# Attention and a routed MoE in one kernel: first scale, table zeros, sums, table steps, values and exponentials moved in program order

## The chip, the cores and the metric

The kernel runs on one core of a Trainium2 chip, in one launch. The metric is the device time of one execution in microseconds (us); lower is better. The core's engines work side by side, each through its own queue in program order, and wait for one another through semaphores: PE (TensorE: matrix products and transposes; its weight loads are listed apart, as PEld), ACT (ScalarE), DVE (VectorE), POOL (GpSimd) and SP (SyncE, which here only issues DMA transfers). DMA transfers are issued from SP, ACT or POOL and move data between device memory and the on-chip buffer.

## The reference

```python
def _attn_ref(q, k, v, cap):                    # q, k, v: (4, 12, 448, 64), float32
    scores = np.matmul(q, k.transpose(0, 1, 3, 2)) / np.sqrt(64)
    scores = cap * np.tanh(scores / cap)
    attn = np.exp(scores - scores.max(-1, keepdims=True))
    attn = attn / (attn.sum(-1, keepdims=True) + 1e-09)
    return np.matmul(attn, v)

def _moe_ref(x, w_gate, w_output_gate, w1, w2):  # x: (1792, 768), 8 experts, F = 1024
    logits = x @ w_gate
    e_idx = np.argmax(logits, axis=1)
    gate_w = softmax(logits)[rows, e_idx]        # abridged
    eom = 1.0 / (1.0 + np.exp(-(x @ w_output_gate)))
    for e in range(8):                           # each row goes through its own expert alone
        mask = e_idx == e
        ye = np.maximum(x[mask] @ w1[e], 0.0) @ w2[e]
        out[mask] = gate_w[mask, None] * eom[mask, e, None] * ye
```

`x` is the attention's output, laid out as one row of 12 heads x 64 for each of the 4 x 448 positions.

## The kernel before

**Attention.** The work is cut into 24 units (`NU`), six for each of the four batches; a unit is two heads. A unit `u` goes through these steps. Its keys and queries are turned so that the head dimension lies on the partitions, and split into a high and a low plane (`K..H`, `K..L`, `QH`, `QL`): a copy (the high plane) and a subtraction (the low plane, `minus`). Units 0 to 2 are turned by PE (`nat_k`, `nat_q`, which read `raw2`), all later ones by DVE (`t_k`, `t_q`, line 288); `TURN` says how many of these turns stand in a unit ahead of its exponential and how many behind. `qk(u, s)` makes four tiles of scores in a ring of three banks, and ACT takes tanh of each into `pt` (line 393, with the scale `icap`). `expo(u)` takes the exponential of the whole unit on ACT (line 396). `pv(u)` multiplies by the values `vv` on PE (line 404) and `u_evac` copies the product out. `presum(u, 0)` and `presum(u, 1)` add a unit's exponentials up in four instructions (lines 413, 414 and twice 418) for the denominators; they run on POOL, for units 20 and later on DVE. `sums` finishes them on PE. `pt` has two buffers, so the tanh of unit `u + 2` overwrites the exponentials of unit `u` and waits until `pv(u)` and `presum(u)` have read them.

**The order of the work** is written out by hand (`manual_schedule`): each engine runs its instructions in the order in which the loop over `u` emits them. In a unit: `load_v`, `qk`, turns, `presum(u - 1, 1)`, slots f and g, `expo(u)`, slot h, `pv(u - 1)`, `sums`, slot q, `u_evac(u - 1)`, turns, `presum(u, 0)`, slot e. The slots hold the steps of the batch that ended before (`end_of_batch`): denominators, gate products, logits, choice of the expert (`choose`), rank among the rows of one expert (`rank_mm`, `place`, `place2`), the weight of a row (`enter`), `scatter` (which enters each row into tables `tabs` in device memory), and six times `row_tr`, `row_out` (the attention's rows, scaled and stored to `xs` by SP). The slots of batch 2 fall into units 19 to 23.

**From attention to MoE.** `early()` is six steps of small DVE instructions that turn the counts of batches 0 to 2 into the experts and table offsets of the first five blocks of 128 rows (`meta`). After it SP reads `meta` and issues `fetch_dma` (the table's entries, `tc`), `load_raw` (the expert's weights into `raw1`, `raw2`); POOL adds the entries up and gathers the block's rows (`gather`, `xg`, line 864). In the last units `first_hi` and `first_lo` split the first weight tile on DVE. PE then turns the first block (`tx(0)`, line 876), ACT and DVE split it (`xh`, `xl`, lines 877 and 878) and every weight tile (lines 1062 and 1063), and PE multiplies (line 1084). The last batch's own steps (`STEPS`) are strewn between the chunks of the first MoE products.

**At the start** SP and ACT load unit 0, DVE fills constants (lines 198 to 203, 256 to 259), and `first_planes` makes the planes of unit 0; `scales` makes `icap`. After unit 0's last scores POOL issues `load_wg` (the gates' weights) and `clear_tabs` (five transfers of zeros from `tabi` to `xs` and the tables).

Of the kernel before, what the change touches and what calls it, by code (L numbers as in the profile page):

```python
# [22 lines left out]
def tile_kernel(ctx: ExitStack, tc, q, k, v, cap, w_gate, w_ogate, w1, w2, out):  # L23
    nc = tc.nc
    B, H, S, D = q.shape
    NT, DM = out.shape
# [3 lines left out]
    NP = H // 2  # L30
    NU = B * NP
# [3 lines left out]
    NE = 5  # L35
# [14 lines left out]
    for i, kind in enumerate((2, 4)):  # L50
# [6 lines left out]
    SP0 = 3  # L57
    UACT = 8
    TURN = {0: (0, 0), 1: (0, 0), 3: (2, 1), 5: (2, 1), 6: (2, 1), 7: (2, 1), 9: (2, 1), 10: (1, 0), 11: (1, 0), 13: (2, 1),
            14: (2, 1), 15: (2, 1), 16: (1, 0), 17: (1, 0), 19: (1, 0), 20: (1, 0), 21: (0, 0)}  # L60
    KD = DM // 128
    KF = DFF // 128
    PB = 5
# [35 lines left out]
    NK = 3  # L99
# [72 lines left out]
    def scales():  # L172
        nc.vector.reciprocal(out=icap, in_=capc)
        nc.vector.tensor_scalar(out=icap, in0=icap, scalar1=float(D) ** -0.5, scalar2=None, op0=ALU.mult)

        nc.vector.tensor_scalar(out=epsc, in0=capc, scalar1=-1.0, scalar2=None, op0=ALU.mult)
        nc.vector.tensor_tensor(out=epsc, in0=epsc, in1=capc, op=ALU.min)

# [14 lines left out]


    ohc = rtp.tile([128, NP, 32], F32, name="ohc")
    nc.vector.memset(ohc, 0.0)
    for p in range(NP):
        nc.vector.memset(ohc[:, p, p:p + 1], 1.0)  # L200

    wg = rtp.tile([128, NP, 2, 16], F32, name="wg")
    nc.vector.memset(wg, 0.0)

    def load_wg():
        for j in range(2):
# [8 lines left out]
    onesb = rtp.tile([CP, 128], BF16, name="onesb")  # L215
    nc.gpsimd.memset(onesb, 1.0)
    tabi = rtp.tile([128, NTAB // 128, 2], F32, name="tabi")

    def clear_tabs():
        nc.gpsimd.dma_start(out=xs[NT:NT + 8].rearrange("r (a m) -> (r a) m", a=16),  # L220
# [33 lines left out]
        nc.gpsimd.memset(wrow[:, 1, COL[r]], 128.0 / KIND[r] - 64.0)  # L254

    part = const.tile([128, 4], F32, name="part")
    for g in range(4):
        for z, x in enumerate((2 * NT + g // 2, 4 * NT + g, 6 * NT + g, 6 * NT + 4 + g)):
            nc.vector.memset(part[32 * g:32 * g + 32, z:z + 1], float(x))
    ereg = const.tile([1, E], F32, name="ereg")  # L260
    nc.gpsimd.iota(ereg, pattern=[[REG, E]], base=128, channel_multiplier=0,
                   allow_small_or_imprecise_dtypes=True)
# [9 lines left out]
    pl, pt, ut, s1, ups, smt, rec, xr, lg = {}, {}, {}, {}, {}, {}, {}, {}, {}  # L272

    def copy(act, dst, src):
        if act:
            nc.scalar.activation(out=dst, in_=src, func=ACTF.Copy)
        else:
            nc.vector.tensor_copy(out=dst, in_=src)
# [4 lines left out]
    def minus(out, x, y):  # L283
        nc.vector.tensor_tensor(out=out, in0=x, in1=y.bitcast(F32), op=ALU.subtract)
# [6 lines left out]
    def q_parts(u, ps):  # L291
        hi, lo = part_tile("QH", [128, S]), part_tile("QL", [128, S])
        return [hi, lo], [(hi, lo, ps)]

    def k_parts(u, ps):
        hi, lo = kpl[u % PB]
        parts = [(hi[:, 0:SK], lo[:, 0:SK], ps[:, 0:SK])]
        for j in range(2):
            h, c = slice(64 * j, 64 * j + 64), slice(SK + 64 * j, SK + 64 * j + 64)
            parts.append((hi[h, c], lo[h, c], ps[h, SK:S]))  # L300
        return [hi, lo], parts

    def planes_of(made):
        ts, parts = made
        for x, _, y in parts:
            copy(False, x, y)
        for x, z, y in parts:
            minus(z, y, x)
        return ts

    def first_planes(pk, pq):
        k_, (main, *tails) = k_parts(0, pk)
        q_, (q0,) = q_parts(0, pq)
        copy(True, main[0], main[2])
        copy(True, q0[0], q0[2])
        for x, z, y in (main, q0):
            minus(z, y, x)
        for x, z, y in tails:
            copy(False, x, y)
            minus(z, y, x)  # L320
        return k_ + q_

    def t_k(u):
        pl[u] = planes_of(k_parts(u, turned(ldk.pop(u), S)))
# [32 lines left out]
    def nat_k(u):  # L357
        pk = tbank([128, S], "tk0")
        for c in range(NK + 1):
            n = min(128, S - c * 128)  # L360
            nc.tensor.transpose(pk[:, c * 128:c * 128 + n], nat[u][0][0:n, c].rearrange("p j d -> p (j d)"), ident[0:n, 0:n])
        return pk

    def nat_q(u):
        pq = scores("tq0")[:, 0, 0:S]
        for c in range(NCH):
            nc.tensor.transpose(pq[:, c * CP:(c + 1) * CP], nat[u][1][:, c].rearrange("p j d -> p (j d)"), ident[0:CP, 0:CP])
        return pq

    def prep_first():  # L370
        pk = nat_k(0)
        pl[0] = first_planes(pk, nat_q(0))
        scales()

    def qk(u, s):
        KH, KL, QH, QL = pl[u]
# [79 lines left out]
    def end_of_batch(b):  # L456
# [82 lines left out]
        def rank_mm():  # L539

            ps = rt["ps"] = bank([128, 2, NCH, E], "trk")
            ohf = rt["ohb"].rearrange("p c e -> p (c e)")
            nc.tensor.matmul(ps[0:CP, 0].rearrange("p c e -> p (c e)"), lhsT=tri, rhs=ohf, start=True, stop=True)
            nc.tensor.matmul(ps[:, 1].rearrange("p c e -> p (c e)"), lhsT=onesb, rhs=ohf, start=True, stop=True)
            den = rt["den"]
            nc.scalar.activation(out=T("ex"), in_=rt["d"], func=ACTF.Exp)
            nc.scalar.activation(out=den[:, 1], in_=den[:, 1], func=ACTF.Exp, scale=-1.0)
# [59 lines left out]
        L = lambda *fs: (lambda: [f() for f in fs])  # L607
        P = lambda f, *a: (lambda: f(*a))
        rws = [L(P(row_tr, p), P(row_out, p)) for p in range(NP)]
        t = [sums_out, L(sums_tr, recips), L(P(gate_mm, 0), P(gate_out, 0)), L(P(gate_mm, 1), P(gate_out, 1))]  # L610
        gts = [L(P(gate_tr, g), P(gate_mul, g)) for g in range(2)]
        g0, g1 = t[2], t[3]
        if b < B - 2:
            at = {(-2, "q"): [g0], (0, "q"): [g1], (0, "e"): [sums_out], (1, "g"): [t[1]],
                  (2, "g"): [rws[0], rws[1]], (3, "g"): gts, (3, "h"): [logits], (4, "g"): [rws[2], rws[3]], (4, "h"): [choose],
                  (5, "g"): [rank_mm, place, rws[4]], (5, "h"): [place2, enter], (6, "g"): [rws[5]]}
            for i, x in enumerate(((6, "g"), (8, "g"), (9, "g"), (10, "g")) if b == 0 else ((6, "g"),) * NCH):
                at.setdefault(x, []).append(P(scatter, (i,)))
        elif b == B - 2:
            g = early()  # L620
            nx = P(next, g, None)
            lds = [P(load_raw, 0, w, c) for w in range(2) for c in range((KD, KF)[w])]
            fd = [P(fetch_dma, i) for i in range(NE)]
            at = {(-2, "q"): [g0], (0, "f"): [P(sums, EARLY), g1, sums_out], (0, "h"): [t[1], *gts, logits, choose],
                  (1, "g"): [rws[0], rank_mm, place], (1, "h"): [place2, enter, scatter], (1, "q"): [rws[1], rws[2], rws[3], store_rows],
                  (1, "e"): [nx] * 5,
                  (2, "g"): [rws[4], rws[5]], (2, "h"): [nx, P(set_known, NE), store_rows],
                  (2, "q"): [fd[0], fd[1], *lds[:2]],
                  (3, "h"): [P(gather, 0), P(gather, 1), *lds[2:4]], (3, "e"): [fd[2], fd[3], *lds[4:KD]], (4, "f"): lds[KD:]}
        if b < B - 1:  # L630
            for (x, y), fs in at.items():
                for f in fs:
                    slots.setdefault((NP * (b + 1) + 1 + x, y), []).append(f)
            return
        nx = P(next, late_steps, None)
        do = dict(g=t[2], s=L(P(sums, NU - 1), t[0]), S=t[1], G=t[3], x=gts[0], X=gts[1], l=logits, c=choose, r=rank_mm, p=place, q=place2,
                  e=enter, n=nx, z=L(P(set_known, NSLOT), P(fetch_dma, NE)), h=lambda: next(rests(), None))
        do.update({str(p): rws[p] for p in range(NP)})
        return [L(*[do[x] for x in w]) for w in STEPS.split()]
# [320 lines left out]
    def slot(u, y):  # L960
        for f in slots.pop((u, y), ()):
            f()

    prep_first()
    warm(WARM[1])
    load_ahead(NN + 1)
    slots.setdefault((2, "f"), []).append(eps)

    for u in range(NU):
        if u % 2:  # L970
            load_v(u + 1)
        for s in range(NK):
            qk(u, s)
        if u == 0:
            pl[1] = planes_of(k_parts(1, nat_k(1)))
        if u > 0:
            load_ahead()
        qk(u, NK)
        if u == 0:
            pl[1] += planes_of(q_parts(1, nat_q(1)))  # L980
            nc.vector.memset(tabi, 0.0)
            load_wg()
            clear_tabs()
        if u == 1:
            pl[2] = planes_of(k_parts(2, nat_k(2)))
            pl[2] += planes_of(q_parts(2, nat_q(2)))
        before, after = TURN.get(u, (2, 0))
        turn_next(before)
        if 0 < u <= NU - 4:
            presum(u - 1, 1)  # L990
        slot(u, "f")
        slot(u, "g")
        expo(u)
        if u > NU - 4:
            presum(u - 1, 0)
            presum(u - 1, 1)
        slot(u, "h")
        if u > 0:
            for c in range(NK + 1):
                pv(u - 1, c)  # L1000
        if u > 1 and u - 2 != EARLY:
            sums(u - 2)
        slot(u, "q")
        if u > 0:
            u_evac(u - 1)
        turn_next(after)
        if u < NU - 4:
            presum(u, 0)
        slot(u, "e")
        store_rows()  # L1010
    u = NU - 1
# [348 lines left out]
```

## Time and profile before

| what | us |
|---|---|
| median of 3 runs (514.47 to 514.91) | 514.79 |
| the profiled execution | 514.19 |
| its span, first to last instruction | 512.6 |
| PE busy | 488.6 (95%) |
| DVE busy | 381.3 (74%) |
| ACT busy | 371.7 (73%) |
| POOL busy | 288.8 (56%) |

The profiled execution took 1.6 us more than its span. Shares are means over two very different stages: attention runs to about 202 us, the MoE from there to the end. The mean granted clock of TensorE is 0.994 of full speed.

### The profile page before, as it was taken

How to read it: one execution, taken by the hardware profiler on the slowest of the kernel's cores; microseconds unless marked ns; L12 is line 12 of the kernel's file. 1: busy time of each engine (PE TensorE's matmuls, PEld its weight loads, DVE VectorE, ACT ScalarE, POOL GpSimd, SP SyncE). 2: the span in 40 equal slices, each digit the busy share in tenths (PEclk: the TensorE clock that was granted, in tenths of full speed). 3: DMA queues.
4: the chain of work that ended last, by engine and by line, in shares of the span. 5: the costliest groups of instructions: out<-in, count | busy, mean ns of one | idle time of the engine just before them, and what ended most of it. 6: DMA issues, size and time to landing. Idle time of an engine off the chain costs nothing. (4 is left out here: it accounts for less than half of the span.)

```text
span 512.6 us, 10021 instructions
## 1 busy us (share of the span) xinstructions
PE 488.6 (95%) x3069; PEld 341.1 (67%) x3069; DVE 381.3 (74%) x746; ACT 371.7 (73%) x433; POOL 288.8 (56%) x310
## 2 busy tenths in 40 slices
PE   7899999999999988999999999999999999999994
PEld 6444455444545543678989979988788867686691
DVE  7669999798686897988999878867676857555550
ACT  5888988889887868556589878858676867665551
POOL 4999998888988614962268861317265035352001
PEclk9999999999999989999999999999999999999998
DMA  6879868484532548884099336259759689991001
GB/s 144 168 134 162 142 108 144 91 146 83 87 70 49 86 61 287 316 271 130 2 350 407 115 104 245 62 207 368 272 191 394 263 308 362 336 359 67 1 33 49
DMA packets 152380, 91.92 MB, mean 179 GB/s; under 512 B 135027, under 2 KB 135163, under 8 KB 152321
## 3 DMA queue, kind: packets, MB, share of 16 engines
q1 hardware_dynamic: 142336, 58.24, 43.6%
q0 software_dynamic: 8832, 32.74, 17.3%
q8 instruction: 26, 0.43, 0.4%
q10 hardware_dynamic: 1152, 0.25, 0.2%
q14 instruction: 34, 0.27, 0.2%
HBM read 123.68 MB, written 12.04 MB: 265 GB/s over the span
## 5 line engine op out<-in xcount | busy, mean ns | idle before, releaser
L1063 DVE TENSOR_TENSOR wr<-raw,wr 128x768 fp32r<-128x768 f32 (+1 forms) x167 | 172.8, 1073 | 64.4 <-ACT wr L1062 63.5
L1062 ACT ACTIVATE wr<-raw 128x768 fp32r<-128x768 f32 (+1 forms) x167 | 150.6, 936 | 28.1 <-PE py L1084 12.4
L393 ACT ACTIVATE pt<-s,icap 128x896 f32<-128x896 f32 x96 | 80.1, 914 | 17.1 <-PE s L386 9.9
L404 PE MATMUL u<-pt,vv 128*64 128x448 f32 x384 | 79.1, 555 | 1.5 <-ACT pt L393 1.1
L1084 PE MATMUL py<-wr,hh 128*128 128x384 f32 x352 | 77.3, 340 | 0.0
L1084 PE MATMUL php<-wr,xh 128*128 128x512 f32 x264 | 74.8, 404 | 0.0
L1153 POOL DMA_INDIRECT out_dram<-yo,ti x13 | 21.7, 1668 | 90.8 <-ACT yo L1151 67.4
L396 ACT ACTIVATE pt<-pt,capc 128x3136 f32<-128x3136 f32 x24 | 69.9, 2912 | 0.6
L1084 PEld LDWEIGHTS py<-wr,hh 128*128 128x128 f32 x352 | 61.2, 188 | 4.0 <-issue 3.7
L1084 PEld LDWEIGHTS php<-wr,xh 128*128 128x128 f32 x264 | 47.4, 188 | 12.8 <-issue 2.5
L418 POOL TENSOR_TENSOR pb<-pb,pt 64x448 f32<-64x448 f32 x42 | 49.6, 1181 | 10.1 <-DVE pb L414 7.0
L404 PEld LDWEIGHTS u<-pt,vv 128*64 128x64 f32 x384 | 25.9, 139 | 42.6 <-issue 34.7
L413 POOL TENSOR_TENSOR pa<-pt 128x896 f32<-128x896 f32 x20 | 42.3, 2114 | 10.8 <-ACT pt L396 10.0
L1084 PE MATMUL py<-wr,hl 128*128 128x384 f32 x176 | 44.8, 335 | 0.0
L414 POOL TENSOR_TENSOR pb<-pa,pt 128x896 f32<-128x896 f32 x20 | 42.1, 2103 | 1.6
L1084 PE MATMUL php<-wr,xl 128*128 128x512 f32 x132 | 41.6, 396 | 0.9 <-DVE xl L878 0.9
L1084 PEld LDWEIGHTS py<-wr,hl 128*128 128x128 f32 x176 | 31.8, 188 | 0.0
L1200 POOL DMA_DIRECT2D rh<-in_moe_w_dram x42 | 23.2, 557 | 15.0 <-DVE wr L1063 8.9
L1084 PEld LDWEIGHTS php<-wr,xl 128*128 128x128 f32 x132 | 24.7, 187 | 7.3 <-DVE xl L878 1.3
L288 DVE STREAM_TRANSPOSE tk<-raw 128x448 f32<-128x448 f32 x42 | 27.5, 654 | 0.9
L1254 POOL DMA_INDIRECT out_dram<-yh,toh x6 | 6.1, 1011 | 35.5 <-issue 13.9
L591 DVE TENSOR_TENSOR xr<-trow,rec 112x512 f32<-112x512 f32 x24 | 16.1, 687 | 10.7 <-PE trow L586 9.7
(315 smaller groups left out, 812.2 us busy)
## 6 DMA issues: line engine op xcount, KB each, us to landing
raw<-in_moe_w_dram SPq DMA_DIRECT2D x78, 512.0 KB
raw<-in_moe_w_dram SPq DMA_DIRECT2D x104, 384.0 KB
rh<-in_moe_w_dram POOLq DMA_DIRECT2D x18, 512.0 KB, 7.2
rh<-in_moe_w_dram POOLq DMA_DIRECT2D x24, 384.0 KB, 8.6
raw<-in_q_dram SPq DMA_DIRECT2D x45, 112.0 KB
vv<-in_v_dram SPq DMA_DIRECT2D x48, 96.0 KB
raw<-in_k_dram SPq DMA_DIRECT2D x40, 112.0 KB
xs<-xr SPq DMA_DIRECT2D x36, 112.0 KB
```

The source lines that it names most:

```text
L288: nc.vector.transpose(out=ps, in_=src.rearrange("p r a -> p (r a)"))
L393: nc.scalar.activation(out=pt[u][:, 2 * s:2 * s + n], in_=ps, func=ACTF.Tanh, scale=icap)
L396: nc.scalar.activation(out=pt[u], in_=pt[u], func=ACTF.Exp, scale=capc)
L404: nc.tensor.matmul(ups[u][64 * j:64 * j + 64], lhsT=V[:, c, j, :], rhs=P[:, 2 * c + (j if c < NK else 0)], start=(c == 0), stop=(c == NK))
L413: eng.tensor_tensor(out=a, in0=P[:, 0:2], in1=P[:, 2:4], op=ALU.add)
L414: eng.tensor_tensor(out=s1[u], in0=a, in1=P[:, 4:6], op=ALU.add)
L418: eng.tensor_tensor(out=s1[u][h, j], in0=s1[u][h, j], in1=P[h, 2 * NK], op=ALU.add)
L1062: nc.scalar.activation(out=t[:, 0, 0:F], in_=raw, func=ACTF.Copy)
L1063: nc.vector.tensor_tensor(out=t[:, 1, 0:F], in0=raw, in1=t[:, 0, 0:F].bitcast(F32), op=ALU.subtract)
L1084: nc.tensor.matmul(ps[g][:, 0:n], lhsT=st[:, c], rhs=w[:, z, g * n:(g + 1) * n], start=(c == 0 and st is hi and z == 0), stop=(c == (KD, K ...
L1153: nc.gpsimd.indirect_dma_start(out=out, out_offset=bass.IndirectOffsetOnAxis(ap=ti, axis=0), in_=y, in_offset=None, bounds_check=NT - 1, o ...
L1200: nc.gpsimd.dma_start(out=d, in_=rows_of(src, e, w, c), **kw)
```

## The change

It moves instructions in program order, some of them to another engine; the arithmetic is the same.

- **Opening.** `first_planes` now serves units 0, 1 and 2: it makes the main part of the keys, then the queries, and the keys' four small tail instructions last. `scales` stands between unit 0's two subtractions; its second half is a function of its own (`eps_of`), behind them. The 23 constant fills of `ohc` and `part` move from DVE's start to the end of unit 0 (`late_consts`); the fills of `wg` and `tabi` move from DVE to POOL's start.
- **Sums.** `presum` of units 20, 21 and 22 moves from the following unit, behind its exponential, to the end of its own unit. The last two turns (unit 23) move from unit 22 to units 20 and 21, since `TURN` gives unit 19 one turn more.
- **Table steps.** Five of the six steps of `early()` move from the end of unit 20 into slot h of unit 21, behind the last two rows of batch 2.
- **Values.** `load_v(22)` moves from the start of unit 21 into its slot h, behind the stores of these rows. The first two weight loads move ahead of the second `fetch_dma`.
- **Exponentials.** For the last batch the two small exponentials of `rank_mm` move behind `place2` (`exps`).

```diff
     TURN = {0: (0, 0), 1: (0, 0), 3: (2, 1), 5: (2, 1), 6: (2, 1), 7: (2, 1), 9: (2, 1), 10: (1, 0), 11: (1, 0), 13: (2, 1),
-            14: (2, 1), 15: (2, 1), 16: (1, 0), 17: (1, 0), 19: (1, 0), 20: (1, 0), 21: (0, 0)}
+            14: (2, 1), 15: (2, 1), 16: (1, 0), 17: (1, 0), 20: (1, 0), 21: (0, 1), 22: (0, 0)}
...
         nc.vector.reciprocal(out=icap, in_=capc)
         nc.vector.tensor_scalar(out=icap, in0=icap, scalar1=float(D) ** -0.5, scalar2=None, op0=ALU.mult)
+    def eps_of():
         nc.vector.tensor_scalar(out=epsc, in0=capc, scalar1=-1.0, scalar2=None, op0=ALU.mult)
         nc.vector.tensor_tensor(out=epsc, in0=epsc, in1=capc, op=ALU.min)
...
     ohc = rtp.tile([128, NP, 32], F32, name="ohc")
-    nc.vector.memset(ohc, 0.0)
-    for p in range(NP):
-        nc.vector.memset(ohc[:, p, p:p + 1], 1.0)
...
-    nc.vector.memset(wg, 0.0)
+    nc.gpsimd.memset(wg, 0.0)
...
     tabi = rtp.tile([128, NTAB // 128, 2], F32, name="tabi")
+    nc.gpsimd.memset(tabi, 0.0)
...
     part = const.tile([128, 4], F32, name="part")
-    for g in range(4):
-        for z, x in enumerate((2 * NT + g // 2, 4 * NT + g, 6 * NT + g, 6 * NT + 4 + g)):
-            nc.vector.memset(part[32 * g:32 * g + 32, z:z + 1], float(x))
+
+    def late_consts():
+        nc.vector.memset(ohc, 0.0)
+        for p in range(NP):
+            nc.vector.memset(ohc[:, p, p:p + 1], 1.0)
+        for g in range(4):
+            for z, x in enumerate((2 * NT + g // 2, 4 * NT + g, 6 * NT + g, 6 * NT + 4 + g)):
+                nc.vector.memset(part[32 * g:32 * g + 32, z:z + 1], float(x))
...
-    def first_planes(pk, pq):
-        k_, (main, *tails) = k_parts(0, pk)
-        q_, (q0,) = q_parts(0, pq)
-        copy(True, main[0], main[2])
-        copy(True, q0[0], q0[2])
-        for x, z, y in (main, q0):
-            minus(z, y, x)
+    def first_planes(u, mid=lambda: None):
+        ts, (main, *tails) = k_parts(u, nat_k(u))
+        if u:
+            copy(False, main[0], main[2])
+            minus(main[1], main[2], main[0])
+        mid()
+        q_, (q0,) = q_parts(u, nat_q(u))
+        if u:
+            copy(False, q0[0], q0[2])
+        else:
+            copy(True, main[0], main[2])
+            copy(True, q0[0], q0[2])
+            minus(main[1], main[2], main[0])
+            scales()
+        minus(q0[1], q0[2], q0[0])
         for x, z, y in tails:
             copy(False, x, y)
             minus(z, y, x)
-        return k_ + q_
+        pl[u] = ts + q_
...
+            if b < B - 1:
+                exps()
+
+        def exps():
             den = rt["den"]
             nc.scalar.activation(out=T("ex"), in_=rt["d"], func=ACTF.Exp)
             nc.scalar.activation(out=den[:, 1], in_=den[:, 1], func=ACTF.Exp, scale=-1.0)
...
-                  (1, "e"): [nx] * 5,
-                  (2, "g"): [rws[4], rws[5]], (2, "h"): [nx, P(set_known, NE), store_rows],
-                  (2, "q"): [fd[0], fd[1], *lds[:2]],
+                  (2, "g"): [rws[4], rws[5]], (2, "h"): [store_rows, P(load_v, NU - 2), *[nx] * 6, P(set_known, NE)],
+                  (2, "q"): [fd[0], *lds[:2], fd[1]],
                   (3, "h"): [P(gather, 0), P(gather, 1), *lds[2:4]], (3, "e"): [fd[2], fd[3], *lds[4:KD]], (4, "f"): lds[KD:]}
...
-        do = dict(g=t[2], s=L(P(sums, NU - 1), t[0]), S=t[1], G=t[3], x=gts[0], X=gts[1], l=logits, c=choose, r=rank_mm, p=place, q=place2,
+        do = dict(g=t[2], s=L(P(sums, NU - 1), t[0]), S=t[1], G=t[3], x=gts[0], X=gts[1], l=logits, c=choose, r=rank_mm, p=place, q=L(place2, exps),
...
-    prep_first()
+    first_planes(0)
+    eps_of()
     warm(WARM[1])
     load_ahead(NN + 1)
     slots.setdefault((2, "f"), []).append(eps)
...
     for u in range(NU):
-        if u % 2:
+        if u % 2 and u < NU - 3:
             load_v(u + 1)
         for s in range(NK):
             qk(u, s)
-        if u == 0:
-            pl[1] = planes_of(k_parts(1, nat_k(1)))
         if u > 0:
             load_ahead()
-        qk(u, NK)
         if u == 0:
-            pl[1] += planes_of(q_parts(1, nat_q(1)))
-            nc.vector.memset(tabi, 0.0)
+            first_planes(1, lambda: qk(0, NK))
+        else:
+            qk(u, NK)
+        if u == 0:
+            late_consts()
             load_wg()
             clear_tabs()
         if u == 1:
-            pl[2] = planes_of(k_parts(2, nat_k(2)))
-            pl[2] += planes_of(q_parts(2, nat_q(2)))
+            first_planes(2)
...
         expo(u)
-        if u > NU - 4:
-            presum(u - 1, 0)
-            presum(u - 1, 1)
         slot(u, "h")
...
         if u > 0:
             u_evac(u - 1)
         turn_next(after)
-        if u < NU - 4:
+        if u < NU - 1:
             presum(u, 0)
+        if NU - 4 <= u < NU - 1:
+            presum(u, 1)
         slot(u, "e")
         store_rows()
```

## Rows read from the trace of the kernel before

**Rows 1.** Busy time of each engine (x instructions) in three stretches, with clock and DMA.

```profile
core 0: us, PE busy (x) PEld busy (x) DVE busy (x) ACT busy (x) POOL busy (x), PEclk, DMA share, GB/s
15.00:30.00 15.00, 12.90 (x82) 7.32 (x82) 9.69 (x23) 12.46 (x13) 14.37 (x11) 1.00 0.87 165
...
184.00:188.00 4.00, 3.19 (x11) 1.27 (x13) 3.80 (x11) 3.97 (x5) 0.00 (x0) 0.71 0.53 103
...
240.00:300.00 60.00, 60.00 (x330) 55.22 (x329) 55.12 (x98) 47.52 (x62) 37.43 (x41) 1.00 0.53 196
```

**Rows 2.** Timeline (start, us, instruction, [idle before <-releaser]), from unit 0's planes to tanh.

```profile
5.40 0.49 ACT L276 ACTIVATE K0H<-tk 128x384 fp32r<-128x384 f32 x1 [0.55 <-PE tk L361]
...
6.30 0.56 DVE L284 TENSOR_TENSOR K0L<-tk,K0H 128x384 fp32r<-128x384 f32 x1
...
7.45 0.47 PE L386 MATMUL s<-QL,K0H 64*128 64x448 f32 x2
...
8.30 0.16 DVE L173 RECIPROCAL icap<-capc 128x1 f32<-128x1 f32 x1
...
8.75 3.33 ACT L393 ACTIVATE pt<-s,icap 128x896 f32<-128x896 f32 x4 [2.16 <-DVE epsc L178]
```

**Rows 3.** Timeline, POOL's zeros and first sums, and the tanh of unit 2.

```profile
12.12 2.92 ACT L396 ACTIVATE pt<-pt,capc 128x3136 f32<-128x3136 f32 x1
...
13.63 0.60 POOL L220 DMA_DIRECT2D xs<-tabi  x1 [4.50 <-DVE tabi L981]
...
16.38 2.11 POOL L413 TENSOR_TENSOR pa<-pt 128x896 f32<-128x896 f32 x1
...
20.76 2.35 POOL L418 TENSOR_TENSOR pb<-pb,pt 64x448 f32<-64x448 f32 x2
...
21.00 0.47 PE L386 MATMUL s<-QH,K2H 64*128 64x448 f32 x2
...
23.15 3.33 ACT L393 ACTIVATE pt<-s,icap 128x896 f32<-128x896 f32 x4 [1.96 <-PE s L386]
```

**Rows 4.** Timeline of DVE from the last steps of unit 20 to unit 22.

```profile
171.77 1.89 DVE L591 TENSOR_TENSOR xr<-trow,rec 112x512 f32<-112x512 f32 x3 [0.64 <-PE trow L586]
...
178.93 1.29 DVE L591 TENSOR_TENSOR xr<-trow,rec 112x512 f32<-112x512 f32 x2 [0.96 <-DMA xs<-xr]
...
180.13 1.08 DVE L413 TENSOR_TENSOR pa<-pt 128x896 f32<-128x896 f32 x1
...
184.15 0.64 DVE L288 STREAM_TRANSPOSE tk<-raw 128x448 f32<-128x448 f32 x1
```

**Rows 5.** Timeline of ACT, the tanh of units 22 and 23.

```profile
183.72 3.33 ACT L393 ACTIVATE pt<-s,icap 128x896 f32<-128x896 f32 x4 [2.93 <-DVE pb L418]
...
192.34 3.33 ACT L393 ACTIVATE pt<-s,icap 128x896 f32<-128x896 f32 x4 [1.16 <-DVE pb L418]
```

**Rows 6.** Timeline, SP's and POOL's way to the first gathered block.

```profile
175.65 1.01 SPq L110 DMA_DIRECT2D vv<-in_v_dram  x2
...
185.93 4.84 SPq L849 DMA_DIRECT2D tc<-tab  x8
...
192.35 1.14 POOL L864 DMA_INDIRECT xg<-xs,ti  x1 [0.66 <-DMA tc<-tab]
```

**Rows 7.** POOL's three gathers from 188 to 215 us, issue to landing.

```profile
DMA to landing us min/median/max: 5.8/6.2/7.5
```

**Rows 8.** Timeline, PE and one ACT wait, from unit 22 to the first MoE blocks.

```profile
184.78 0.47 PE L391 MATMUL s<-QH,K2H 128*128 128x448 f32 x1 [1.67 <-ACT pt L393]
...
198.67 3.23 PE L404 MATMUL u<-pt,vv 128*64 128x448 f32 x16 [0.25 <-ACT pt L396]
...
205.59 0.74 PE L1084 MATMUL php<-wr,xl 128*128 128x512 f32 x2 [0.89 <-DVE xl L878]
...
222.55 0.21 ACT L547 ACTIVATE den<-den 112x4 f32<-112x4 f32 x1 [2.50 <-DVE den L537]
...
225.87 0.41 PE L876 MATMUL pt_x<-ident,xg 128*128 128x128 f32 x2 [1.17 <-DVE rk L556]
```

More of the change, by code (lines that the diff above doesn't have):

```diff
@@ L368, in nat_q @@
         return pq
[L370 to L373, printed above, removed]
     def qk(u, s):
```

## Prediction

> **What bounds the kernel now.** I read the busy time by stage first, then the timelines wherever an engine stood idle, one engine at a time, and asked of each gap what ended it. Behind 240 us PE has no gap at all (60.00 of 60.00 us) [rows 1]; nothing that the change touches there can be worth much, but whatever lets the MoE start earlier is kept to the end. So the question is how early PE gets there, and three places ahead of it have gaps.
>
> The first is the opening. ACT stands idle for 2.16 us until 8.75, when `icap` exists [rows 2]. But ACT is not what paces the next stretch: POOL is busy for 14.37 of 15 us between 15 and 30 us [rows 1]. It begins unit 0's sums at 16.38, although the exponential that they add up ended at 15.04 (12.12 + 2.92); until then it issues zeros, from 13.63, where it had waited 4.50 us for DVE's fill of `tabi` [rows 3]. The tanh of unit 2 overwrites what these sums read. They end at 23.11 (20.76 + 2.35) and that tanh starts at 23.15 after 1.96 us of idling. The row names PE as releaser, but its scores, begun at 21.00, take about 1 us (an estimate: three pairs of matmuls like the row's); POOL came last.
>
> The second is unit 22. POOL is idle there, and DVE is the queue that all wait for: its tanh starts 2.93 us late and that of unit 23 1.16 us late, both released by DVE's sums [rows 5]. DVE's order is what to see in [rows 4]: the last rows end at 173.66, then stand five table steps, then two rows that first wait 0.96 us for an earlier store to leave their buffer (until 178.93), and only then unit 20's sums (180.13 to about 183.7), the sixth step, two turns from 184.15, and unit 21's sums until just ahead of 192.34 [rows 5].
>
> The third is the MoE's start. PE waits 0.89 us for `xl`, DVE again, and 1.17 us at 225.87 for DVE's `rk` [rows 8].
>
> **The change, part by part.** Times are those of before; what an earlier part gives back is taken off at the end.
>
> *Opening.* `scales` comes ahead of the query's subtraction. The reciprocal takes 0.16 us [rows 2]; with the like instruction behind it, which waits for its result, I count 0.35. DVE has the room: the fills in front of the first subtraction are gone, so that starts when the key copy ends at 5.89 instead of 6.30. `QL` is thus ready when it was, the last pair of the first tile's matmuls runs from 7.45 to 7.92 [rows 2], and tanh can start at about 8.07 instead of 8.75: 0.68 earlier. The 23 fills land on DVE behind unit 1's planes, where it next waits for PE; cost nothing there.
>
> POOL gains more. Its two new fills have 192 and 242 columns; the nearest row, an addition over 896, took 2.11 us [rows 3], which bounds each; by columns I take 0.3 each. Before, the gates' loads were issued by 9.13 (13.63 - 4.50) and the zeros took 2.75 (13.63 to 16.38) [rows 3]; without the wait for DVE both are out by 12.5 even if nothing comes sooner, ahead of the first exponential's end at 15.04 - 0.68 = 14.36. Unit 0's sums start then instead of 16.38, 2.0 earlier, and end at 21.1; PE's scores for unit 2, also 0.68 earlier, let its tanh start at about 21.3. POOL's sums pace units 3 to 5, so the 2.0 us are kept there, and further on the chain tanh, scores, `pv`, next scores hands them down. Bounds: 0.68 if POOL's lead were spent on PE at once, 2.0 if all is kept. I take **1.95**, since POOL was almost without a pause. The zeros now run beside the loads of unit 2 and of the first values, on DMA engines that were 0.87 busy at 15 to 30 us anyway [rows 1]; they leave that stretch instead.
>
> *Turns.* The two turns of unit 22 took 4.6 us: 184.15 to 192.3, less 3.6 for unit 21's sums, as long as unit 20's [rows 4, 5]. I give the keys 2.6 and the queries 2.0, an estimate by their instructions (seven and three). In the new order unit 19 has the queries of 22 more, and unit 20 the keys of 23 in place of them, 0.6 more, in front of the rows at 171.77, which had 0.64 us to spare [rows 4]. Cost: nothing; without that cover 0.6.
>
> *Sums and table steps.* DVE's new order behind 173.66: unit 20's sums (3.5 us) until 177.2; rows 4 and 5, which still wait for the stores; then six table steps: five took 4.3 us (173.66 to 177.97, where the 0.96 of waiting began) and the sixth about 0.5 more (to 184.15); one turn (the query's, 2.0 us); unit 21's sums, 3.5 us. The stores were waited for until 178.93. Behind them now lie no value loads, which may bring them sooner: between 177.2 and 178.9, I take 178.2. Then: rows 179.6, steps 184.6, turn 186.6, sums 190.1. So the tanh of unit 23 starts at 190.1 instead of 192.34: **2.2 earlier**, bounds 1.6 (store at 178.9) and 2.9 (177.2). The tanh of unit 22, no longer behind DVE, starts between 180.8 (183.72 - 2.93) and 183.72, so ACT itself is not later than 190.5 at worst and probably done earlier [rows 5].
>
> *The MoE's start.* `pv` of unit 23 shifts with that tanh from 198.67 to 196.4 [rows 8]. DVE now has unit 22's sums behind it, not in front of the first split, and is some 4 us ahead, against 2.2 for PE: the 0.89 us for `xl` go. **0.9**.
>
> *Values and fetches on SP.* In front of the first `fetch_dma` (185.93) [rows 6] SP now has four row stores, the six loads of `load_v(22)` and the six table steps. By the order above `meta` is ready at about 185; before, the same ten transfers were issued from 175.65 on [rows 6], the values first; now they start with the stores at 179.6, but need not wait for rows any more. I take the fetch at 186.3, +0.4. The gather then starts at 192.4 or so and lands up to 7.5 later [rows 6, 7], at 199.9; but fewer weights lie ahead of it, two loads being 2 us out of the way by then, so I take 198.5. PE wants it at 199.7. Cost nothing, with 1.2 us of cover at most; each us beyond that is a us lost. The values are needed by `pv` of unit 22 near 192: covered.
>
> *Exponentials.* ACT waited 2.50 us for `den` with the next weight split behind it in the queue, and DVE's subtraction and then `rk` behind that [rows 8]. Without it that split can start when PE frees its buffer, about 0.9 sooner; DVE has a row in between, so PE's 1.17 shrink by **0.6** (bounds 0 and 1.17).
>
> **The clock.** At 184 to 188 us the granted clock was 0.71 [rows 1]: full speed (2.4 GHz), then a stretch at 1.2 GHz that began after PE had stood idle 1.67 us in front of 184.78 [rows 8]. It cost nothing, for DVE was later. In the new order PE stands idle in front of unit 23's fourth score tile for about 1.7 us as well, from the end of its scores to 190.1 + 1.0. If the clock falls there, `pv` of unit 22 (3.23 us like [rows 8]'s) runs at half speed in front of `pv` of unit 23, with little room: 1.3 us lost. The Trainium skill ("TensorE: Matmul & The Clock Gate", Part 1) says that the array is throttled by default and that only recent activity lifts this; by that rule the fall follows the idle time to its new place, and the sum would be 1.3 us smaller. The trace bears the rule out once, in this place; the mean clock of 0.994 leaves room for little more than this one fall.
>
> **The sum.** 1.95 + 2.2 + 0.9 + 0.6 = 5.65 us off 514.19: 508.5 for an execution like the profiled one, which is 0.6 below the median of the runs: 509.2 as a median.
>
> **Rivals.** (a) *The clock falls* in unit 23, as above: 4.3 us, 510.5. For it: the same idle time was followed by it before. Against: that is one case, and the idle time gets shorter if the stores land early. (b) *The opening gives only its 0.68*: zeros and gate weights collide with the loads of unit 2 and the first values, or another queue holds unit 2's tanh. 4.4 us, 510.4. For it: DMA 0.87 busy [rows 1]. Against: no row names a wait for these loads. (c) *The gather is late*: slower than before. The ten transfers took SP from 175.65 to 185.9 before, waits included [rows 6]; if they take as long again from 179.6, the fetch starts near 189.9 and PE waits for the tile. It decides from 190.5 on: then the tile lands at 204.4 (199.85, by 192.35 and 7.5 [rows 6, 7], and 4.55 later), 2.5 later than PE wanted it before (201.9), which eats the opening's 1.95 and the 0.6. At 192.5 it is 2 us slower: 516.8. (d) *DVE's order changes nothing* since the store's wait moves along with it, and the opening's lead is lost to PE: no change, 514.8.
>
> **How the numbers follow.** Forecast 0.55, with 507.8 to 510.2 as its own range (2.0 + 2.9 + 0.9 + 1.17 at best, 1.9 + 1.6 + 0.9 + 0.2 at worst, off 514.8). (a) 0.18, (b) 0.10, (a) and (b) or a half-late gather together 0.05 (512.0), (c) 0.07, (d) 0.05. The range reaches from 507.7 to 512.2, to take in (a), (b) and their sum. One measurement of this kernel tells 0.2%, about 1.0 us, from no change. Faster by more: 0.88; within: 0.05; slower: 0.07.
>
> **What would show it.** The first tanh at 8.1 and POOL's first addition at 14.4, unit 2's tanh near 21.3; unit 20's sums directly behind row 3 on DVE, at about 171.7 on the new clock; unit 23's tanh released near 188.1; the first `fetch_dma` near 184.3; no wait for `xl` at the first MoE chunk; the granted clock in unit 23. The prediction is wrong if `icap` waits for the load of `cap`, which no row of before prices; if the first gather lands behind `pv` of unit 23; or if PE's idle time only moves into the first MoE chunks.

## Result, and the profile after

The changed kernel takes 510.26 us (median of six runs, 509.15 to 510.94) against 514.63 beside it: ratio 0.9913, 95% interval 0.9896 to 0.9930, so 4.4 us faster. Forecast were 5.6; 510.26 lies in the range, just outside the forecast's own (507.8 to 510.2). The profiled execution takes 509.4 us, its span 507.8 against 512.6: 4.8 less, which can be followed through the trace.

The stretches that answer to [rows 1], and the one in which PE now waits:

```profile
15.00:30.00 15.00, 13.75 (x84) 7.79 (x85) 10.96 (x28) 13.78 (x13) 14.38 (x9) 1.00 0.85 143
184.00:188.00 4.00, 3.81 (x28) 1.82 (x22) 3.79 (x6) 3.04 (x2) 0.00 (x0) 1.00 0.25 42
188.00:190.00 2.00, 0.63 (x3) 0.48 (x3) 1.86 (x3) 1.69 (x2) 1.47 (x2) 1.00 0.53 109
240.00:300.00 60.00, 60.00 (x326) 54.62 (x325) 54.40 (x84) 47.10 (x61) 38.69 (x46) 1.00 0.56 202
```

The timeline of the changed kernel (all engines, in order of time), for [rows 2] to [rows 8]:

```profile
6.75 0.54 ACT L278 ACTIVATE QH<-tq 128x448 fp32r<-128x448 f32 x1 [0.51 <-PE tq L377]
...
7.68 0.60 POOL L217 DMA_DIRECT2D xs<-tabi  x1
...
8.52 3.34 ACT L398 ACTIVATE pt<-s,icap 128x896 f32<-128x896 f32 x4 [1.23 <-PE s L391]
...
14.89 2.09 POOL L418 TENSOR_TENSOR pa<-pt 128x896 f32<-128x896 f32 x1 [4.49 <-ACT pt L401]
...
21.78 3.33 ACT L398 ACTIVATE pt<-s,icap 128x896 f32<-128x896 f32 x4 [0.81 <-PE s L391]
...
49.78 3.33 ACT L398 ACTIVATE pt<-s,icap 128x896 f32<-128x896 f32 x4 [0.32 <-PE s L391]
...
172.01 1.08 DVE L418 TENSOR_TENSOR pa<-pt 128x896 f32<-128x896 f32 x1
...
176.76 1.29 DVE L600 TENSOR_TENSOR xr<-trow,rec 112x512 f32<-112x512 f32 x2 [1.25 <-DMA xs<-xr]
...
184.63 1.08 DVE L418 TENSOR_TENSOR pa<-pt 128x896 f32<-128x896 f32 x1
184.80 2.14 SPq L857 DMA_DIRECT2D tc<-tab  x4
...
188.31 3.33 ACT L398 ACTIVATE pt<-s,icap 128x896 f32<-128x896 f32 x4 [1.27 <-DVE pb L423]
189.37 0.47 PE L396 MATMUL s<-QH,K3H 128*128 128x448 f32 x1 [1.41 <-ACT pt L398]
194.63 3.23 PE L409 MATMUL u<-pt,vv 128*64 128x448 f32 x16 [0.25 <-ACT pt L401]
197.79 0.87 PE L884 MATMUL pt_x<-ident,xg 128*128 128x128 f32 x6
...
198.26 16.54 SPq L834 DMA_DIRECT2D raw<-in_moe_w_dram  x17
...
203.50 1.06 ACT L1069 ACTIVATE wr<-raw 128x1024 fp32r<-128x1024 f32 x1 [1.83 <-DMA raw<-in_moe_w_dram]
...
207.88 0.65 PE L480 MATMUL trec<-ident,ssb 128*112 128x128 f32 x4 [1.17 <-DVE xl L886]
...
220.10 0.60 PE L884 MATMUL pt_x<-ident,xg 128*128 128x128 f32 x4
221.17 0.41 PE L884 MATMUL pt_x<-ident,xg 128*128 128x128 f32 x2 [0.47 <-DVE rk L565]
```

Of the kernel before, for comparison: the copy of the first query tile, the tanh of unit 6, and PE's transposes of the first MoE tile and of the third:

```profile
6.05 0.54 ACT L276 ACTIVATE QH<-tq 128x448 fp32r<-128x448 f32 x1 [0.16 <-PE tq L367]
...
51.33 3.33 ACT L393 ACTIVATE pt<-s,icap 128x896 f32<-128x896 f32 x4 [0.30 <-PE s L386]
...
201.83 0.87 PE L876 MATMUL pt_x<-ident,xg 128*128 128x128 f32 x6
...
224.10 0.60 PE L876 MATMUL pt_x<-ident,xg 128*128 128x128 f32 x4
```

Rows 0 to 5 in the text are the six `row_out` steps of the third batch (batch 2). Read from the top. POOL's zeros no longer wait; its first addition starts at 14.89, released by the exponential and 1.49 earlier than in [rows 3]. Unit 2's tanh is 1.37 earlier, that of unit 6 (49.78) 1.55. Unit 20's sums stand behind row 3, and unit 23's tanh is 4.03 earlier than in [rows 5], 2.48 of it beyond the opening. `pv` of unit 23 and the first MoE transposes keep 4.04. Then something new: ACT waits 1.83 us at 203.50 for a chunk of weights, and through the split, DVE and `xl` PE waits 1.17 us at 207.88, where it had waited 0.89 two chunks earlier [rows 8]; the third tile's transposes (220.10) are 4.00 earlier. PE's wait for `rk` fell from 1.17 to 0.47; that last pair of transposes is 4.70 earlier.

### The profile page after: what moved, and what is told of

It reads as the page before. It is cut to its first block, busy times and chain, and to the rows that moved or that the text cites. A ratio compares the mean times of both kernels' runs of the same rounds, so it can differ in the third digit from the quotient of the medians.

```text
span 507.8 us, 10022 instructions
## 1 busy us (share of the span) xinstructions
PE 487.2 (96%) x3069; PEld 341.5 (67%) x3069; DVE 381.4 (75%) x744; ACT 371.2 (73%) x433; POOL 290.2 (57%) x312
## 5 line engine op out<-in xcount | busy, mean ns | idle before, releaser
L409 PE MATMUL u<-pt,vv 128*64 128x448 f32 x384 | 77.5, 545 | 1.5 <-ACT pt L398 1.1
L586 POOL DMA_INDIRECT tab<-ent,posi x16 | 17.0, 1062 | 13.3 <-DVE ent L578 8.9
```

Of the source, the lines that this page charges most:

```text
L409: nc.tensor.matmul(ups[u][64 * j:64 * j + 64], lhsT=V[:, c, j, :], rhs=P[:, 2 * c + (j if c < NK else 0)], start=(c == 0), stop=(c == NK))
```

## Experiments

Every kernel is measured beside the kernel before on the same chip; ratios are to that, and kernels of different chips are compared by their ratios (the changed kernel itself did not run beside the first four, nor beside the last four). The first theory: three separate gains (opening, sums at unit 23, exponentials) add up, and a late load of weights takes the fourth. Its rivals stand with the runs.

**The opening undone** (the late part alone: sums, table steps, values, exponentials): `scales()` behind the query's subtraction, fills of `ohc`, `wg`, `part` and `tabi` on DVE, zeros behind DVE's fill.

> The changed kernel with the whole opening as before: scales behind the query's subtraction, the fills of ohc, wg, part and tabi on DVE, zeros issued behind DVE's fill; everything from unit 3 on as changed. Theory (the opening is worth the 1.56 us by which unit 6's tanh came earlier, and all of it reaches the end): first tanh near 8.75, POOL's first addition near 16.4, unit 2's tanh near 23.1, unit 23's tanh near 189.9, time 1.5 longer, about 511.8. Rival (the later parts hide some of it, as unit 23 waits for DVE and DVE for its stores): unit 6's tanh 1.5 later but unit 23's by 0.5 at most, time 510.8 at most.

514.47 us, 0.9980 (0.9964 to 0.9996). First tanh 8.80, unit 2's 23.21, unit 6's 51.34: the opening's part is as expected. But the late part alone gains 1.0 us only, and unit 23's tanh is at 193.84, worse than before:

```profile
168.00:172.00 4.00, 3.51 (x12) 1.25 (x13) 2.93 (x12) 3.64 (x5) 3.81 (x3) 0.62 0.29 57
```

In this execution the clock fell in unit 20 (mean 0.62, so partly 1.2 GHz), unit 21's tanh came 2.46 later than in the kernel before (173.51), and rows 4 and 5 waited 1.91 and 0.77 us for their stores. Why the clock fell there is open. It fell once more in unit 23 (0.58 at 198 to 200 us), behind 2.91 us of idling. The late part alone (1.0) and the opening alone (2.2, below) make 3.2 us, not 4.4: the gains don't simply add up, and how much of the rest is the clock's is open too.

**Zeros late.** `late_consts(); nc.vector.memset(tabi, 0.0)` in place of the fill on POOL.

> One edit of the changed kernel undone: tabi is filled by DVE behind unit 1's planes again, so POOL's zeros wait for DVE there; scales stay ahead. Theory (POOL's lead is what the opening gave): first tanh stays near 8.5, zeros near 13.4, POOL's first addition near 16.2 instead of 14.89, unit 2's tanh near 23.0 instead of 21.78, time 1.3 longer, 511.6. Rival (the lead came from the scale and unit 1's planes; POOL's late start is made up by unit 5): unit 6's tanh 0.5 later at most, time 510.3 to 510.7.

516.44 us, 1.0014 (0.9994 to 1.0033): slower than expected, for a reason that the rows of POOL and DVE show:

```profile
14.87 0.26 DVE L990 MEMSET tabi<- 128x242 f32 x1
...
15.42 0.60 POOL L216 DMA_DIRECT2D xs<-tabi  x1 [7.95 <-DVE tabi L990]
...
18.18 2.12 POOL L417 TENSOR_TENSOR pa<-pt 128x896 f32<-128x896 f32 x1
```

Behind the 23 late fills the fill of `tabi` lets the zeros start at 15.42, even later than in [rows 3]. POOL's addition starts 3.29 later than in the changed kernel, and unit 6's tanh (53.49) is 3.71 later although the first tanh, 8.47, is not. So POOL's first addition sets the opening: over before, after and these two runs it starts at 16.38, 14.89, 16.43 and 18.18, and unit 6's tanh follows 34.95, 34.89, 34.91 and 35.31 later. The extra 0.4 here goes with a fall of the clock (mean 0.70 at 24 to 28 us) behind the longer wait for POOL. By the ratios this run is 5.2 us over the changed kernel; where the 1.5 beyond unit 6's 3.71 come from is not shown: in the trace row 4 waited 2.09 us for its store, the clock fell in unit 23, and that unit's tanh is at 193.80.

**Exponentials early.** `rank_mm` ends with `exps()` for the last batch too; `q=place2`.

> One edit of the changed kernel undone: the last batch's two exponentials stand in rank_mm again, ahead of the weight splits on ACT. Theory (ACT's wait for den held up a split and through DVE rk): PE's wait ahead of pt_x grows from 0.47 to about 1.1, time 0.55 longer, 510.8. Rival (PE's wait there is DVE's own, or what it loses there it would lose behind): wait under 0.6, time within 0.2 of 510.3.

512.94 us, 0.9939 (0.9918 to 0.9960), some 1.3 over the changed kernel by the ratios. PE:

```profile
222.21 0.60 PE L883 MATMUL pt_x<-ident,xg 128*128 128x128 f32 x4
223.98 0.41 PE L883 MATMUL pt_x<-ident,xg 128*128 128x128 f32 x2 [1.17 <-DVE rk L564]
```

From the first to the second line 1.77 us, against 1.07 in the changed kernel: the exponentials are worth 0.70. The rest of the 1.3 is not read from them: already 40 us ahead of the edit rows 4 and 5 waited 1.91 and 1.41 us here (the second wait is put down to PE), unit 23's tanh was at 190.67, and the clock fell behind it.

**Sums in their old place.** `presum(u - 1, 0)` and `(u - 1, 1)` behind `expo(u)` for units 21 to 23, none at the unit's end.

> One edit of the changed kernel undone: the sums of units 20 to 22 stand behind the next unit's exponential again, so on DVE behind rows 4 and 5 of the third batch and, for unit 22, behind the last score tile's unit. Table steps, turns, values and exponentials stay as changed. Theory (unit 23's tanh is set by DVE's order, which now holds the sums, steps, turn and sums behind the wait for the stores): the sums of unit 20 start behind the rows at about 178, all that follows is 3 later, unit 23's tanh near 191.5 instead of 188.31, time 3 to 3.5 longer, 513.3 to 513.8. Rival (ACT or PE is as late there as DVE): unit 23's tanh under 1 later, time under 511.5.

514.81 us, 0.9972 (0.9951 to 0.9993): 3.0 over the changed kernel by the ratios. The wait for the stores comes first and the sums behind it:

```profile
176.29 0.69 DVE L600 TENSOR_TENSOR xr<-trow,rec 112x512 f32<-112x512 f32 x1 [3.81 <-DMA xs<-xr]
178.68 0.69 DVE L600 TENSOR_TENSOR xr<-trow,rec 112x512 f32<-112x512 f32 x1 [1.70 <-DMA xs<-xr]
179.29 1.08 DVE L418 TENSOR_TENSOR pa<-pt 128x896 f32<-128x896 f32 x1
...
193.16 2.80 ACT L398 ACTIVATE pt<-s,icap 128x896 f32<-128x896 f32 x3 [3.58 <-DVE pb L423]
```

The theory holds: DVE's order sets unit 23. But in this trace the clock fell too (0.50 at 194 to 200 us), and the first MoE transposes came 12.10 us behind that tanh instead of 9.48; how much of the 3.0 is the clock's is not told apart. The wait for the stores differs from run to run, so the next runs ask what it is worth.

**The changed kernel again**, no edit.

> The changed kernel with no edit, beside the others of its call. Theory (in the single edits, rows 4 and 5 of the third batch waited longer for the stores than in the first trace of the changed kernel, unit 23's tanh came 2.4 later for that, and PE idled near 2.9 us there with the clock falling behind it): this happens with no edit too in some executions; first tanh 8.0 to 8.5, unit 6's tanh 49.3 to 49.8, rows 4 and 5 at 176.7 to 179.7, unit 23's tanh between 188.3 and 190.7, time 510 to 512.5. Rival (the edits themselves shifted the stores): rows at 176.8, unit 23's tanh at 188.3 and time 509.2 to 511.

511.53 us against 515.81, 0.9915 (0.9885 to 0.9945): the same ratio as at first. Its profile:

```profile
178.27 0.69 DVE L600 TENSOR_TENSOR xr<-trow,rec 112x512 f32<-112x512 f32 x1 [2.17 <-DMA xs<-xr]
180.40 0.69 DVE L600 TENSOR_TENSOR xr<-trow,rec 112x512 f32<-112x512 f32 x1 [1.44 <-DMA xs<-xr]
...
186.78 2.14 SPq L857 DMA_DIRECT2D tc<-tab  x4
...
191.33 3.33 ACT L398 ACTIVATE pt<-s,icap 128x896 f32<-128x896 f32 x4 [3.47 <-DVE pb L423]
192.39 0.47 PE L396 MATMUL s<-QH,K3H 128*128 128x448 f32 x1 [2.91 <-ACT pt L398]
```

So with no edit at all row 4 starts 1.5 us later than in the first trace and row 5 some 3 later, both behind stores (row 3 itself is 0.6 later), and unit 23's tanh comes 3.0 later. Why they do is open.

**Own buffers.** Rows 4 and 5 of the third batch don't share a buffer with an earlier row:

```python
            if b == B - 2 and p >= 4:
                x = raw2[p + 2][0:CP, 0:NCH * 128].rearrange("p (c m) -> p c m", c=NCH)
            else:
                x = xrp.tile([CP, NCH, 128], F32, tag=f"xr{nrow[0] % 3}", name="xr")
```

> Rows 4 and 5 of the third batch are written to two buffers of their own (the weight buffers that nothing uses then), so they don't wait for an earlier row's store. Theory (the store's landing sets the table steps and so unit 23's tanh): rows 4 and 5 directly behind unit 20's sums at about 175.5, table steps at 176.8, unit 23's tanh near 187.1, PE idle under 0.5 there and the clock at full speed; what reaches the end is 1.2 where the store was 1.25 late and up to 3.5 where it was later, less what the weights' loads take back. Rival (another wait is as late: unit 22's scores or exponential, or the stores' landing ahead of the gather): unit 23's tanh as in the unedited run, time within 0.5 of it.

509.28 us, 0.9899 (0.9857 to 0.9941).

```profile
176.51 0.14 DVE L660 TENSOR_TENSOR bcnt<-pre,ereg 1x8 f32<-1x8 f32 x1
...
183.62 2.14 SPq L860 DMA_DIRECT2D tc<-tab  x4
...
186.84 3.33 ACT L398 ACTIVATE pt<-s,icap 128x896 f32<-128x896 f32 x4
...
202.07 1.06 ACT L1072 ACTIVATE wr<-raw 128x1024 fp32r<-128x1024 f32 x1 [1.86 <-DMA raw<-in_moe_w_dram]
...
206.61 0.65 PE L480 MATMUL trec<-ident,ssb 128*112 128x128 f32 x4 [1.36 <-DVE xl L889]
```

No wait for a store and none of ACT ahead of unit 23; that tanh is 1.47 earlier than in the first trace of the changed kernel and 4.49 earlier than in the second. PE's wait for the weights, though, is still there.

**Steps ahead of the rows.** `(1, "e"): [nx] * 6` in place of the six in `(2, "h")`.

> The six table steps stand ahead of rows 4 and 5 of the third batch on DVE (behind unit 20's sums), where they fill the wait for the stores; the sums stay where the change put them. Theory (DVE's order sets unit 23's tanh): steps at 175.5, rows at about 180.4 without a wait, unit 23's tanh near 187.1, as with own buffers, while the last stores, values and the first fetch come 2 later on SP, which is the price at the MoE's start: the first gathered tile up to 1 late. Rival (the later stores hold the first gather by more than that): PE waits 2 us or more for the tile, time not shorter than unedited.

516.62 us, 1.0007 (0.9985 to 1.0030): the whole gain is gone.

```profile
188.66 2.14 SPq L858 DMA_DIRECT2D tc<-tab  x4
...
189.41 3.31 ACT L398 ACTIVATE pt<-s,icap 128x896 f32<-128x896 f32 x4
...
209.69 1.45 POOL L423 TENSOR_TENSOR pb<-pb,pt 64x448 f32<-64x448 f32 x1 [4.14 <-DMA raw<-in_moe_w_dram]
...
211.20 1.70 PE L442 MATMUL sm<-pb,ohc 128*32 128x448 f32 x2 [4.66 <-POOL pb L423]
```

The rival's time came, though not by the wait that it named, for the first tile. The last stores, the values and the first fetch are 3.9 later on SP. Unit 23's last additions (the second half of its `presum` runs on POOL, not on DVE) stand behind the second gather there, and PE waits 4.66 us for them. Nor is unit 23's tanh at 187.1: unit 22's came at 182.81 already, because PE had waited 1.53 us for row 4.

**Weights ahead.** `(3, "e"): [*lds[4:KD], fd[2], fd[3]]` instead of `[fd[2], fd[3], *lds[4:KD]]`.

> The last two chunks of the first block's weights are loaded ahead of the fetches for blocks 2 and 3 instead of behind them: 4.6 us earlier on SP. Theory (in the first trace of the changed kernel the late fifth chunk cost ACT 1.83 and PE 1.17 us and gave the MoE start's gain back): no wait of ACT for raw and none of PE for xl near 205 to 208; the stretch from the first transposes of the MoE to those of the third tile is 20.9 us instead of 22.3; time up to 1.2 shorter than unedited where that wait was there, same where it wasn't. Rival (the chunks collide with the first gather): PE waits for the gathered tile, time same or longer.

511.99 us, 0.9931 (0.9905 to 0.9957): no gain. The wait at 203 is gone, a like one stands 5.5 us further on,

```profile
209.05 2.01 ACT L1069 ACTIVATE wr<-raw 128x1024 fp32r<-128x1024 f32 x2 [1.86 <-DMA raw<-in_moe_w_dram]
```

and from the first MoE transposes (198.98) to those of the third tile (221.82) it takes 22.84 us, not 20.9.

**Own buffers and weights.** Both, with five chunks ahead: `[*lds[4:KD + 3], fd[2], fd[3]]`.

> Own buffers for rows 4 and 5, and besides five of the ten weight chunks still to be loaded stand ahead of the fetches for blocks 2 and 3. Theory (what is left at the MoE's start is the order in which SP issues the weights' loads): no wait of ACT for raw up to 209, none of PE for xl, the stretch from the first transposes to those of the third tile 20.9 instead of 22.3, time 1 to 1.4 under that of own buffers alone. Rival (the DMA engines are full from 190 on, so a load that comes sooner makes another late: the gathers, or the chunks behind): that stretch stays at 22 or more, POOL's wait for xg grows past 2, time same or longer than with own buffers alone.

510.41 us against 514.69, 0.9926 (0.9906 to 0.9945), no shorter than own buffers alone beside it (0.9903). The rival again: with the weights sooner the second gather lands 6.4 us after its issue instead of 4.2 with own buffers alone,

```profile
202.66 1.61 POOL L423 TENSOR_TENSOR pb<-pb,pt 64x448 f32<-64x448 f32 x1 [4.30 <-DMA xg<-xs,ti]
...
204.33 0.94 PE L442 MATMUL sm<-pb,ohc 128*32 128x448 f32 x2 [1.80 <-POOL pb L423]
```

and that stretch takes 24.24 us (195.82 to 220.06). So a sooner place on SP is no gain here either.

**Values first.** `if u % 2:` ahead of `load_v(u + 1)` again, and no `load_v` behind the stores.

> One edit of the changed kernel undone: the six loads of the last two units' values stand on SP at the start of unit 21 again, ahead of the last row stores. Theory (SP had room, both orders cost nothing): the last four stores start up to 2 later, the first fetch stays within 0.5 of 184.8 or the gather's 1.2 of cover takes it up, unit 23's tanh unchanged, time within 0.5 of 511.5. Rival (the values on the DMA engines hold the stores that rows 4 and 5 wait for, or the later stores hold the first gather, as with the steps ahead of the rows): rows 4 and 5 up to 1 later or the first fetch past 187, time 1 to 4 longer.

509.90 us, 0.9904 (0.9890 to 0.9918): moving the values cost and gave nothing that can be told. The fetch is at 184.07. In this trace the clock fell in unit 23:

```profile
188.00:190.00 2.00, 0.22 (x3) 0.17 (x2) 1.83 (x4) 1.23 (x2) 1.72 (x3) 1.00 0.82 256
190.00:192.00 2.00, 1.98 (x7) 0.75 (x9) 1.95 (x3) 2.00 (x3) 1.83 (x1) 0.72 0.85 283
192.00:194.00 2.00, 2.00 (x8) 0.72 (x6) 1.94 (x3) 1.97 (x2) 0.84 (x2) 0.50 0.92 332
```

```profile
190.73 4.92 PE L409 MATMUL u<-pt,vv 128*64 128x448 f32 x16
...
199.63 0.87 PE L884 MATMUL pt_x<-ident,xg 128*128 128x128 f32 x6
```

From unit 23's first tanh (188.77) to the first MoE transposes it takes 10.86 us, against 9.48 in the changed kernel's first trace: rival (a), at 1.38 where 1.3 was forecast. But the third tile's transposes are at 220.50, 0.40 behind that trace's, and the tanh had been 0.46 behind: the 1.38 don't arrive, because here ACT waits for no weights up to there.

**The opening alone**, on the kernel before.

> The kernel before with the change's opening alone (scales, fills, zeros, unit 1's planes, late constants); sums, turns, table steps, values, fetch order and exponentials as before. Theory (what the opening gains is handed down to the end): first tanh 8.0 to 8.7, unit 6's tanh 1.3 to 2.0 earlier than before's 51.33, unit 23's tanh as much earlier than 192.34, time 1.3 to 2.0 under before's median of the same call. Rival (the waits for stores around unit 22 do not move with it, so it is lost there): unit 23's tanh at 192 or later, time within 0.5 of before.

512.47 us, 0.9960 (0.9947 to 0.9973): 2.2 under 514.69. First tanh 8.18, unit 6's 49.48, and

```profile
190.43 3.33 ACT L398 ACTIVATE pt<-s,icap 128x896 f32<-128x896 f32 x4 [1.92 <-DVE pb L423]
```

1.91 earlier than in [rows 5]: the opening is handed down whole.

**Own buffers again.**

> Own buffers for rows 4 and 5 once more, beside the kernel that also moves the weights. Theory: unit 23's tanh between 186.4 and 187.4, no fall of the clock behind 184, time 508 to 510.5, 5 to 7 under before's median of the same call. Rival (the first time's 509.28 was a matter of the chip): unit 23's tanh past 188 or the time above 511.

508.54 us, 0.9903 (0.9869 to 0.9936); unit 23's tanh at 186.56, first fetch at 183.56, PE's wait for `xl` 1.90. Own buffers give the shortest traces (spans 506.8 and 506.9), but one or two of six runs each took over 512 us, and by the intervals it isn't settled that they beat the changed kernel.

## Why the prediction came out as it did

**Opening, 1.95: right.** Alone it gave 2.2 us in time and 1.91 at unit 23. The first profile of the changed kernel shows 1.55 at unit 6, since the query's first tile was copied 0.70 later there (6.75 for 6.05). From that copy to the first tanh it takes 1.77 us instead of 2.70, so the scale was worth 0.9 at an equal start; over all runs with the new opening the tanh starts between 7.73 and 8.74. That POOL paces the rest is shown by the late zeros; and at the tanh of unit 2, where the prediction held POOL to be last against the row's PE, the run with the opening undone names POOL (23.21). Rivals (b), 0.68 only, and (d), no change, fell.

**Sums and table steps, 2.2: right in place and size, but not in every execution.** Unit 23's tanh gained 2.48 beyond the opening. That the sums' move carries it is shown by undoing it (that tanh at 193.16, 3.0 us in time, the clock's part included). The bound, 1.6 at worst, was too narrow: in the changed kernel's second trace the stores landed so late that the tanh gained 1.01 in all, less than the opening alone.

**The MoE's start, 0.9: the step that failed; it gave nothing.** `xl` of the first block no longer waits, as forecast, but the step asked only whether DVE would be done, and the forecast's own range had no bound for it. The fifth chunk of weights, issued at 198.26 behind the fetches, lands 5.2 us later, and ACT, DVE, `xl` and PE wait for it in turn. From first transposes to the third tile's, the changed kernel takes 22.31 us and the kernel before 22.27. What the prediction named as a sign of being wrong, that PE's idle time only moves within the first MoE chunks, came true for this term. Shown is that a sooner place for the weights on SP is no cure, in two runs. The wait goes with how far PE's first MoE transposes stand behind SP's first fetch. In the traces with that order of loads (steps ahead of the rows aside, where PE waits for POOL) this was 12.48 and 12.71 us with own buffers, 12.99 and 14.03 in the changed kernel, and PE waited 1.90, 1.36, 1.17 and 0.69 us for `xl`. In the other five (values first, exponentials early, opening undone, zeros late, sums in their old place) it was 15.10 to 16.97, PE did not wait, and the stretch took 20.87. So where PE comes early, the MoE's start now follows SP's chain of stores, values, fetches and weights, not DVE; the DMA engines were busy at 0.82 to 1.00 between 190 and 198 in the changed kernel, which fits, but that they are the limit is only argued.

**Exponentials, 0.6: right.** 0.70 between the traces (1.77 us between the third tile's two groups of transposes before, 1.07 after), and 0.70 by the edit undone.

**Values and fetch, nothing: right.** The fetch was forecast at 184.3 and is at 184.80. Rival (c) is a true mechanism: with the steps ahead of the rows the fetch was at 188.66 and the gain was lost; what PE then waits for is POOL's last sums behind the second gather, not the first tile.

**The clock, rival (a): true in some executions, and without a price in the one that was followed to its end.** The clock fell in unit 23 in five of the other traces too and near 209 us in a sixth (steps ahead of the rows), to 0.50 each time. The Trainium skill ("TensorE: Matmul & The Clock Gate", Part 1) says that only recent activity lifts the throttle. The traces agree so far that the fall follows idle time, 1.78 us of it in the one shown; but 1.41 and 2.91 us of idling in unit 23 were followed by no fall in the two traces of the changed kernel, the same 2.91 us by a fall with the opening undone, and no run here shows what decides. Over a whole execution the mean granted clock is 0.995 to 0.998 in the six traces without a fall ahead of 500 us and 0.990 to 0.994 in the eight with one. Of the changed kernel's first six executions only the traced one has 0.998, the others 0.992 to 0.994: most of them probably held a fall that no trace shows. One of these, at 0.992, took 509.15 us, no longer than the traced one.

The sum by the first trace: 1.55 + 2.48 + 0.0 + 0.70 = 4.7 of 4.8 us, against 5.65. Of the 0.95 missing, 0.9 are the MoE's start and 0.4 the opening, less 0.3 that the sums and 0.1 that the exponentials gave more. The stated range holds the result, but it had been widened for the clock and for a poorer opening, not for the weights: in part that is luck.

## What to carry to other kernels

Follow a gain to the next engine that it reaches sooner, and ask there of every input, not only of the one that was late before: PE came 4.0 us sooner to weights whose loads stood only 2.9 sooner on SP (198.26 instead of 201.15). A wait for a DMA in an engine's queue can be met by putting ready work ahead of it, provided that what the transfer's own queue issues behind it isn't pushed back: the same move paid with the sums, and lost everything with the table steps. Take the size of such a wait from several executions.

## What the runs showed of the hardware

The same two rows, in the same program, waited 1.25 us for their stores in one execution and 2.17 and 1.44 in another. With the new opening the copy of the first query tile moved by up to 1.0 us between executions (from 5.96 to 6.97), and POOL's queue, waiting for the first exponential, handed that on (the late zeros aside): its first addition came between 14.09 and 15.11, and unit 6's tanh 34.9 us behind it each time. A stretch at half clock that cost PE 1.38 us had no price at the third tile, where the other trace waited as long for weights. Weight loads issued sooner made another transfer later: the second gather landed 6.4 us after its issue instead of 4.2 with own buffers alone.
